# Fused spectral filter and feed-forward block: paired fold operations, four weight transfers in flight, and residual sums moved between engines

## The chip, the cores and the metric

The kernel runs on one core of one Trainium2 chip. The metric is the device time of one execution in microseconds; the figure quoted is a median over runs. A core has a matrix engine (PE, with its weight loads listed as PEld), a vector engine (DVE, VectorE), an activation engine (ACT, ScalarE), GpSimd (POOL), and a queue engine (SP) that issues nearly all transfers here. They run their own instruction streams in order and meet at semaphores.

## The reference

The input `x` has 2048 rows of 640 bfloat16 values. It is normalised once, and two branches read the result.

```
xn  = layernorm(x)                                   # over the 640 columns
A   = irfft2(rfft2(xn, (rows, cols)) * (w_r + i*w_i))  # filter of 2048 x 321 complex values
B   = gelu(xn @ w1 + b1) @ w2 + b2                   # 640 -> 1536 -> 640
out = x + A + B
```

## The kernel before

The 2048 rows are held as 16 tiles `c` of 128 rows; tile `c` has the rows `16p + c`. All Fourier transforms are matrix products with tables (`gtab`, `etab`, `mtab` forward; `ntab`, `getab`, `htab` back). The stages are:

1. **Normalise and fold** (lines 559 to 615). For each tile VectorE takes statistics (L563, L565), GpSimd makes `rstd` (L566, L567), and VectorE writes the normalised tile `xn` (L576). A transposed copy `xnT` is made through PE for the first eight tiles (L584, copied by L482 or L479) and by transfer for the last eight (L594). VectorE then folds the tile: two sums and differences of a half with the other half reversed (L601, 320 elements each), and four more of the result (L605, 256 and 64 elements). PE multiplies the folded tile with `gtab`, and the product is copied into `XW2`, which the trace calls `XW`.
2. **First product of the feed-forward branch** (`hps`, line 617 on): PE multiplies `w1` and `xnT` in blocks of 1, 1, 2, 4, 4 and 4 tiles, in all 360 matmuls of 128, 256 or 512 columns; ScalarE applies the gelu (L632). This is what fills PE while other stages wait.
3. **Forward transform and filter**: for each of 8 pairs PE runs `etab`, results are copied to `Xb`, PE runs `mtab`, results are copied to `Y`; VectorE multiplies `Y` with the filter weights `Wf` (L688, two per pair), adds the parts into `Z` (L693); small gathers make `Zs`; PE runs `ntab`; the result is copied to `XV`.
4. **Second product and inverse**: for each of 8 pairs `cp` PE runs `getab`, the result is copied into `Wf` (now free), VectorE unfolds it in two steps (L761, L766, two each), and PE adds the `htab` product. The second feed-forward product (`W,gT` in the trace, 24 matmuls of 320 columns for a tile) is the filler of this stage.
5. **Sums**: the first five tiles are "staged": their second product is done before the inverse is there. VectorE adds `b2` to it (L807), GpSimd adds the residual `x` (L810), and VectorE adds the inverse (L816). For the other eleven tiles GpSimd makes `x + b2` (L780), the `htab` product is accumulated onto the second product, and VectorE adds both (L800).

The order on every engine is not written by hand. A planner in the kernel (`Sched`) holds each operation with a guessed duration, a priority from `PRIO`, its buffers and its predecessors, lays the operations out in time on five engines, and emits that order with the semaphore waits it needs. An operation that may run on two engines is given to the one that the plan finds free first. Buffers come from pools (`Pool(n)` has n slots), so an operation can also have to wait for the last reader of a slot. Changing a duration or a dependency anywhere can therefore move operations everywhere.

The filter weights come in 18 transfers of 160.5 KB or less: four of rows of 10,272 bytes for each of `w_r` and `w_i`, then five each that bring the mirrored rows, in pieces of 642 bytes. Each is told to wait for an earlier one:

```
few.append(load(dst, src, B_w, nbytes, after=few[-DEPTH:][:1], rate=rate))
```

SP issues them in one queue with the transposes of tiles 8 to 15.

Of the kernel before, what the change touches and what calls it, by code (L numbers as in the profile page):

```python
# [10 lines left out]
ALU = mybir.AluOpType  # L11

S = 2048
D = 640
F = 1536
H2 = 320
# [82 lines left out]
def mm_us(n):  # L99
    return max(n / 2400.0 + 0.003, 0.0265)  # L100


def dve_us(n, rate=1.0):
    return 0.066 + n / 960.0 / rate


def act_us(n, ptr=0):
    return 0.052 + n / 1200.0 + 0.092 * ptr
# [8 lines left out]
PRIO = {"hps": 10, "gelu": 50, "pb": 70, "pc": 80, "filt": 85, "ipc": 90, "eps": 60, "fin": 40, "fst": 5}  # L117
# [6 lines left out]
DEPTH = 2  # L124
# [262 lines left out]
def bass_parallel_sum__spectral_gfnet__dense_activation_gelu__prompt_kernel(  # L387
# [21 lines left out]
    with ExitStack() as es:  # L409
# [3 lines left out]
        def view(t, off, dims):  # L413
            width = int(np.prod(t.shape[1:]))
            return bass.AP(tensor=t, offset=off, ap=[[width, 128]] + dims)
# [33 lines left out]
        XN, X1, XF = 0, 4 * D, 7 * D  # L449
# [13 lines left out]
        p_xn, p_x1, p_xf, p_xb, p_y, p_t, p_z, p_zs = Pool(8), Pool(3), Pool(4), Pool(2), Pool(2), Pool(2), Pool(2), Pool(2)  # L463
# [94 lines left out]
        norm_ops, ring_ops = [], []  # L558
        for c in range(16):
# [9 lines left out]
            xn, xf = Buf(f"xn{c}", p_xn), Buf(f"xf{c}", p_xf)  # L569

            def xnv(o, dims, xn=xn):
                return view(TT, XN + xn.slot * D + o, dims) if xn.slot < 4 else view(Zb, (xn.slot - 4) * D + o, dims)

            def xfv(o, dims, xf=xf):
                return view(TT, XF + xf.slot * D + o, dims)
            norm_ops.append(K.op([("dve", 0.36)], pr, lambda e, _, c=c, xnv=xnv: e.tensor_scalar(  # L576
                out=xnv(0, [[1, D]]), in0=view(XV, c * D, [[1, D]]), scalar1=mv[:, c, 0:1], scalar2=rstd[:, c:c + 1], op0=ALU.subtract, op1=ALU.mult),
                reads=[B_x[c], B_rs[c], B_mv], writes=[xn]))
            if c < BYPE:
# [6 lines left out]
                ring_ops.append(K.op([("pe", 5 * mm_us(128))], pr, xt, reads=[xn, B_id], writes=[tps]))  # L586
                if c == 0:
                    b1_column(ring_ops[:])
# [7 lines left out]
            x1 = Buf(f"xe{c}", p_x1)  # L596

            def x1v(o, dims, x1=x1):
                return view(TT, X1 + x1.slot * D + o, dims)
            for k, op in enumerate((ALU.add, ALU.subtract)):  # L600
                K.op([("dve", dve_us(H2, 2))], prf, lambda e, _, k=k, op=op, xnv=xnv, x1v=x1v: e.tensor_tensor(  # L601
                    out=x1v(H2 * k, [[1, H2]]), in0=xnv(0, [[1, H2]]), in1=xnv(D - 1, [[-1, H2]]), op=op), reads=[xn], writes=[x1])
            for k, op in enumerate((ALU.add, ALU.subtract)):
                for o_, o0, o1, n in ((128 * k, 0, H2 - 1, 128), (512 + 32 * k, 128, H2 - 129, 32)):
                    K.op([("dve", dve_us(2 * n, 2))], prf, lambda e, _, op=op, x1v=x1v, xfv=xfv, o_=o_, o0=o0, o1=o1, n=n: e.tensor_tensor(  # L605
                        out=xfv(o_, [[2 * n, 2], [1, n]]), in0=x1v(o0, [[H2, 2], [1, n]]), in1=x1v(o1, [[H2, 2], [-1, n]]), op=op),
                        reads=[x1], writes=[xf])
            aps = Buf(f"aps{c}", psum, 2, ZONE["aps"])
            ring_ops.append(K.op([("pe", 5 * mm_us(128))], prf, mms(lambda c=c, xfv=xfv, aps=aps: [
                (ps(aps.slot + j // 4, 128 * (j % 4), 128 * (j % 4) + 128), xfv(128 * j, [[1, 128]]), gtab[:, c, :], True, True) for j in range(5)]),  # L610
                reads=[xf, B_g], writes=[aps]))
            K.op([("dve", dve_us(640)), ("act", act_us(640))], prf,
                 copy(lambda c=c: view(XW2, 4 * c, [[2048, 5], [64, 32], [1, 4]]),
                      lambda aps=aps: PS[aps.slot // 2][:, 0:640].rearrange("p (j q r) -> p j q r", j=5, q=32)),
                 reads=[aps], writes=[B_xa[c]])
# [41 lines left out]
        for pair in range(8):  # L657
# [10 lines left out]
            cps_ops[pair] = [K.op([("pe", 4 * mm_us(KP) + 0.2)], PRIO["pc"] - pair / 5, mms(lambda pair=pair, cps=cps, xb=xb: [  # L668
# [75 lines left out]
        last, fin_ops, st_ops = [], {}, []  # L744
# [4 lines left out]
        for cp in range(8):  # L749
# [20 lines left out]
            for n in range(2):  # L770
# [8 lines left out]
                if not staged:  # L779
                    K.op([("pool", pool_us(640))], 50, lambda e, _, xr=xr, xov=xov: e.tensor_tensor(  # L780
                        out=xov(0, D), in0=xrt[:, xr.slot, :], in1=b2bc[:], op=ALU.add), reads=[xr, B_b2b], writes=[xo], after=[z_last])
# [11 lines left out]
                for hh in range(n_h):  # L793
# [9 lines left out]
                    if staged:  # L803
                        part = []
                        st_ops += second(hs, fps, hps_ops[block_of[c]], True)
                        add = Buf(f"st{c}")
                        K.op([("dve", dve_us(D))], 86, lambda e, _, xov=xov, fps=fps: e.tensor_tensor(  # L807
                            out=xov(0, D).rearrange("p (h n) -> p h n", h=2), in0=ps2(fps.slot, H2), in1=b2bc[:].rearrange("p (h n) -> p h n", h=2), op=ALU.add),
                            reads=[fps, B_b2b], writes=[add], after=all_hps)
                        K.op([("pool", pool_us(640) + 0.3)], 50, lambda e, _, xr=xr, xov=xov: e.tensor_tensor(  # L810
                            out=xov(0, D), in0=xov(0, D), in1=xrt[:, xr.slot, :], op=ALU.add), reads=[xr, add], writes=[xo], after=[z_last])
                        add = xo
# [11 lines left out]
                    K.op([("dve", dve_us(H2 * len(hs)))], 95, total, reads=[fps, add], writes=[os_])  # L824
# [34 lines left out]
```

## Time and profile before

| quantity | value |
|---|---|
| median of 13 runs | 168.27 us (165.93 to 170.16) |
| the profiled execution | 167.34 us, of which the span of the trace is 165.4 us |
| PE busy | 151.0 us (91% of the span) |
| VectorE busy | 120.5 us (73%) |
| ScalarE busy | 81.7 us (49%) |
| GpSimd busy | 36.4 us (22%) |
| granted clock of PE | 1.00 in every slice |

The profile page has the busy time of each engine, the span in 40 slices, the transfers by queue, the chain of work that ended last, and groups of equal instructions with their mean duration and what ended the idle time before them. The trace behind it answers with instructions in order of time, with waits, and with busy time in chosen windows. A duration in the trace contains the pipeline's tail, so for a run of equal instructions the distance from start to start is the better price.

### The profile page before, as it was taken

What the parts mean: (1) busy time and instruction counts of PE and PEld (TensorE: products, weight loads), DVE (VectorE), ACT (ScalarE), POOL (GpSimd) and SP (SyncE); (2) the same over time, 40 slices, a digit from 0 to 9 for tenths busy, and PEclk for the clock granted to TensorE, in tenths of its full rate; (3) what the DMA queues carried; (4) which work ended last, traced back from release to release, by engine and by line L of the source; (5) the groups of instructions that cost most, each with busy time, mean ns of one, the idle gap of its engine ahead of it and who ended that gap; (6) DMA issues with size and microseconds to landing.
All of it is one profiled execution on the core that took longest, in us unless ns stands there. A gap on an engine that the chain in (4) does not pass through costs nothing.

```text
span 165.4 us, 3694 instructions
## 1 busy us (share of the span) xinstructions
PE 151.0 (91%) x1485; PEld 94.9 (57%) x1485; DVE 120.5 (73%) x295; ACT 81.7 (49%) x163; POOL 36.4 (22%) x56
## 2 busy tenths in 40 slices
PE   6899999999999939999999999795699999999993
PEld 2489885444555514445556666563356777777772
DVE  3759999999982184967679988789999782923221
ACT  3299987786576838996889351313424010100000
POOL 1306233233200000000000000892703243333300
PEclk9999999999999999999999999999999999999999
DMA  3999944899995920050513000141524031211111
GB/s 109 352 384 394 296 119 116 135 130 123 87 133 86 159 74 0 0 162 0 162 29 133 0 0 4 40 119 44 164 73 159 23 117 65 84 40 40 42 63 55
DMA packets 18633, 17.86 MB, mean 108 GB/s; under 512 B 6712, under 2 KB 17336, under 8 KB 18488
## 3 DMA queue, kind: packets, MB, share of 16 engines
q1 hardware_dynamic: 18448, 17.59, 44.2%
q8 instruction: 11, 0.18, 0.5%
q10 hardware_dynamic: 168, 0.04, 0.1%
q14 instruction: 6, 0.05, 0.1%
HBM read 13.69 MB, written 2.62 MB: 99 GB/s over the span
## 4 chain that ended last, share of the span: by engine, by line
PE 40%; DVE 29%; DMA 18%; ACT 8%; issue 2%; SPq 2%; DVEq 0%
PE ps L472 40%; DMA Wf<-in_A_w_i_dram 7%; DMA Wf<-in_A_w_r_dram 6%; DVE stats L563 5%; DMA XV<-in_A_x_dram 5%; DVE T L688 4%; DVE T L605 3%; DVE T L576 2%; ACT Xb L479 2%; ACT Zs L479 2%; DVE Wf L761 2%; DVE Z L693 2%; DVE T L601 2%; DVE Wf L766 2%; DVE Y L482 1%
## 5 line engine op out<-in xcount | busy, mean ns | idle before, releaser
L472 PE MATMUL ps<-xnT,W 128*128 128x512 bf16 (+2 forms) x360 | 58.6, 309 | 1.3 <-DVE xnT L482 0.5
L472 PE MATMUL ps<-W,gT 128*128 128x320 bf16 x384 | 56.5, 299 | 0.3 <-DVE xnT L807 0.2
L472 PEld LDWEIGHTS ps<-W,gT 128*128 128x128 bf16 x384 | 36.7, 98 | 15.1 <-DVE xnT L807 0.8
L632 ACT ACTIVATE gT<-ps,b1col 128x512 bf16<-128x512 f32 (+2 forms) x72 | 37.1, 545 | 7.3 <-PE ps L472 6.7
L472 PEld LDWEIGHTS ps<-xnT,W 128*128 128x128 bf16 x360 | 28.1, 98 | 20.1 <-ACT gT L632 2.9
L800 DVE TENSOR_TENSOR ost<-ps,xo 128x640 bf16<-128x640 f32 (+1 forms) x12 | 9.2, 767 | 18.2 <-PE ps L472 18.2
L780 POOL TENSOR_TENSOR xo<-xr,b2bc 128x640 f32<-128x640 bf16 x11 | 16.1, 1466 | 24.7 <-DVE ost L800 24.7
L479 ACT ACTIVATE Wf<-ps 128x640 bf16<-128x640 f32 x12 | 8.0, 702 | 27.1 <-PE ps L472 24.9
L810 POOL TENSOR_TENSOR xnT<-xnT,xr 128x640 f32<-128x640 f32 x5 | 6.9, 1404 | 62.2 <-DVE Z L693 59.3
L563 DVE BATCH_NORM_STATS2 stats<-XV 128x6 f32<-128x320 bf16 x32 | 14.8, 474 | 3.3 <-DMA XV<-in_A_x_dram 3.3
L688 DVE TENSOR_TENSOR T<-Y,Wf 128x1288 bf16<-128x1288 bf16 x16 | 12.7, 828 | 4.1 <-ACT gT L632 3.6
L605 DVE TENSOR_TENSOR T<-T 128x256 bf16<-128x256 bf16 x64 | 11.7, 229 | 0.1
L761 DVE TENSOR_TENSOR Wf<-Wf 128x640 bf16<-128x640 bf16 x16 | 10.8, 702 | 0.2
L472 PE MATMUL ps<-Wf,htab 128*128 128x320 bf16 x32 | 7.2, 300 | 3.6 <-DVE Wf L766 3.4
L479 ACT ACTIVATE Xb<-ps 128x640 bf16<-128x640 f32 x11 | 9.3, 888 | 2.3 <-PE ps L472 2.3
L479 ACT ACTIVATE Zs<-Z 128x128 bf16<-128x128 bf16 (+1 forms) x33 | 6.4, 270 | 8.2 <-DVE Z L693 8.2
L479 ACT ACTIVATE XW<-ps 128x640 bf16<-128x640 f32 x13 | 9.0, 704 | 2.5 <-PE ps L472 2.2
L482 DVE CAST XV<-ps 128x640 bf16<-128x640 f32 x8 | 6.6, 824 | 5.0 <-PE ps L472 5.0
L566 POOL TENSOR_SCALAR ve<-mv 128x1 f32<-128x1 f32 x16 | 3.7, 233 | 29.5 <-DVE mv L565 29.5
L567 POOL TENSOR_TENSOR rstd<-ve,mhalf 128x1 f32<-128x1 f32 x16 | 9.4, 585 | 1.3
L472 PE MATMUL ps<-ntab,Z 64*128 64x128 bf16 x128 | 5.0, 218 | 4.5 <-ACT Xb L479 3.2
L601 DVE TENSOR_TENSOR T<-T 128x320 bf16<-128x320 bf16 x32 | 9.1, 294 | 0.0
(46 smaller groups left out, 147.6 us busy)
## 6 DMA issues: line engine op xcount, KB each, us to landing
W<-in_B_w_dram SPq DMA_DIRECT2D x6, 640.0 KB, 4.9
xr<-in_A_x_dram SPq DMA_DIRECT2D x16, 160.0 KB, 2.3
out_dram<-ost SPq DMA_DIRECT2D x15, 160.0 KB, 1.8
XV<-in_A_x_dram SPq DMA_DIRECT2D x7, 320.0 KB, 9.3
Wf<-in_A_w_r_dram SPq DMA_DIRECT2D x7, 160.5 KB, 5.0
Wf<-in_A_w_i_dram SPq DMA_DIRECT2D x7, 160.5 KB, 3.7
gtab<-c_G SPq DMA_DIRECT2D x1, 512.0 KB, 8.9
htab<-c_H SPq DMA_DIRECT2D x1, 512.0 KB, 10.8
```

What stands on the lines that cost most here:

```text
L472: ins = e.matmul(o_, lhsT=lw, rhs=rh, start=st, stop=sp_)
L479: return e.activation(dst(), src(), ACT.Copy, scale=scale)
L482: return e.tensor_copy(dst(), src())
L563: K.op([("dve", 0.4)], pr, lambda e, _, c=c, h=h: e.bn_stats(stats[:, c, 6 * h:6 * h + 6], view(XV, c * D + H2 * h, [[1, H2]])), reads=[B_ ...
L567: K.op([("pool", 0.6)], pr, lambda e, _, c=c: e.tensor_tensor(out=rstd[:, c:c + 1], in0=ve[:, c:c + 1], in1=mhalf[:, c:c + 1], op=ALU.pow) ...
L601: K.op([("dve", dve_us(H2, 2))], prf, lambda e, _, k=k, op=op, xnv=xnv, x1v=x1v: e.tensor_tensor(out=x1v(H2 * k, [[1, H2]]), in0=xnv(0, [[ ...
L605: K.op([("dve", dve_us(2 * n, 2))], prf, lambda e, _, op=op, x1v=x1v, xfv=xfv, o_=o_, o0=o0, o1=o1, n=n: e.tensor_tensor(out=xfv(o_, [[2 * ...
L632: K.op([("act", act_us(s1 - s0, 1))], pr + PRIO["gelu"], lambda e, _, s0=s0, s1=s1, fc=fc, hps=hps: e.activation(gT[:, fc, s0:s1], ps(hps. ...
L688: t_ops[pair].append(K.op([("dve", dve_us(4 * KP, 2))], pr, lambda e, _, k=k, Y=Y, TB=TB, pair=pair: e.tensor_tensor(out=view(TT, TB.slot ...
L761: K.op([("dve", dve_us(D, 2))], pr + 2, lambda e, _, k=k, op=op, yo=yo, y2=y2: e.tensor_tensor(out=view(Wf, Y2 + y2.slot * 2 * D + (H2 - 1 ...
L780: K.op([("pool", pool_us(640))], 50, lambda e, _, xr=xr, xov=xov: e.tensor_tensor(out=xov(0, D), in0=xrt[:, xr.slot, :], in1=b2bc[:], op=A ...
L800: return e.tensor_tensor(out=ost[:, os_.slot, a:b].rearrange("p (h n) -> p h n", h=len(hs)), in0=ps2(fps.slot, H2)[:, hs[0]:hs[-1] + 1, :] ...
```

## The change

Five things change together.

- **Folds over two tiles.** Tiles are folded in pairs. L601 becomes two instructions of 2 x 320 elements, L605 becomes four of 2 x 256 and 2 x 64, for every two tiles. The slots of `xn`, of the first fold and of the second fold now hold two tiles each: four pair slots of `xn` (it had eight single ones), two of each fold's result.
- **Weights four deep.** `DEPTH` goes from 2 to 4: a filter transfer waits for the one four places earlier.
- **Staged tiles on VectorE.** Residual plus bias of the five staged tiles is made by VectorE ahead of the product (`xpb`, priority 20, once the first product is through), and the product is then added to it; the GpSimd addition L810 is gone.
- **GpSimd paced.** The eleven GpSimd additions of tile `c` wait for the output sum of tile `c - 4`.
- **A planned duration.** The `mtab` step is planned with 0.36 us instead of 0.2 us of extra time, and the staged second products are gated on all of the first product.

```
-DEPTH = 2
+DEPTH = 4
+PACE = 4
...
-        p_xn, p_x1, p_xf, p_xb, p_y, p_t, p_z, p_zs = Pool(8), Pool(3), Pool(4), Pool(2), Pool(2), Pool(2), Pool(2), Pool(2)
+        p_xn, p_x1, p_xf, p_xb, p_y, p_t, p_z, p_zs = Pool(4), Pool(2), Pool(2), Pool(2), Pool(2), Pool(2), Pool(2), Pool(2)
...
             for k, op in enumerate((ALU.add, ALU.subtract)):
-                K.op([("dve", dve_us(H2, 2))], prf, lambda e, _, k=k, op=op, xnv=xnv, x1v=x1v: e.tensor_tensor(
-                    out=x1v(H2 * k, [[1, H2]]), in0=xnv(0, [[1, H2]]), in1=xnv(D - 1, [[-1, H2]]), op=op), reads=[xn], writes=[x1])
+                K.op([("dve", dve_us(D, 2))], prf, lambda e, _, k=k, op=op, xnv=xnv, x1v=x1v: e.tensor_tensor(
+                    out=x1v(H2 * k, [[D, 2], [1, H2]]), in0=xnv(-D, [[D, 2], [1, H2]]), in1=xnv(-1, [[D, 2], [-1, H2]]), op=op), reads=[xn2], writes=[x12])
...
+                if staged:
+                    K.op([("dve", dve_us(D))], PRIO["xb"], lambda e, _, xr=xr, xov=xov: e.tensor_tensor(
+                        out=xov(0, D), in0=xrt[:, xr.slot, :], in1=b2bc[:], op=ALU.add), reads=[xr, B_b2b], writes=[B_xb], after=all_hps)
+                else:
                     K.op([("pool", pool_us(640))], 50, lambda e, _, xr=xr, xov=xov: e.tensor_tensor(
-                        out=xov(0, D), in0=xrt[:, xr.slot, :], in1=b2bc[:], op=ALU.add), reads=[xr, B_b2b], writes=[xo], after=[z_last])
+                        out=xov(0, D), in0=xrt[:, xr.slot, :], in1=b2bc[:], op=ALU.add), reads=[xr, B_b2b], writes=[xo],
+                        after=[z_last] + os_ops[max(c - PACE, 0):][:1])
...
-                        K.op([("pool", pool_us(640) + 0.3)], 50, lambda e, _, xr=xr, xov=xov: e.tensor_tensor(
-                            out=xov(0, D), in0=xov(0, D), in1=xrt[:, xr.slot, :], op=ALU.add), reads=[xr, add], writes=[xo], after=[z_last])
```

As the planner now lays it out, ten of the 512-column matmuls of the first product that stood ahead of the first `etab` step stand behind it (98 ahead before, 88 now); 64 matmuls of the second product stand ahead of the last `ntab` step instead of 92; five of the copies into `XW` after the start-up are on VectorE instead of three; and the transposed copy of tile 1 is on ScalarE, ahead of its table load.

## The prediction

> **What bounds the kernel.** I read first the busy row and the PE row of the slices, then the busy time by stage, then the chain of waits. PE is busy 151.0 of 165.4 us at a granted clock of 1.00, and the 512-column matmuls follow each other every 0.215 us (13 in 2.80 us). The change removes no matmul, so it can only move the 14.4 us in which PE has none. Busy time by stage (length, then PE, weight loads, VectorE, ScalarE, GpSimd) shows where they lie:
>
> ```profile
> 36.00:58.00 22.00, 21.63 (x174) 11.00 (x172) 14.57 (x55) 15.57 (x24) 2.57 (x7) 1.00 1.00 119
> 58.00:62.20 4.20, 1.37 (x7) 0.48 (x5) 3.62 (x7) 1.53 (x6) 0.00 (x0) 1.00 0.19 61
> 62.20:105.00 42.80, 41.47 (x512) 23.78 (x512) 33.81 (x59) 29.61 (x66) 0.93 (x1) 1.00 0.16 47
> 105.00:125.00 20.00, 15.23 (x176) 9.80 (x179) 18.15 (x26) 6.01 (x9) 10.91 (x9) 1.00 0.32 98
> 125.00:163.00 38.00, 37.81 (x305) 27.02 (x304) 19.34 (x32) 2.71 (x4) 11.06 (x8) 1.00 0.21 69
> ```
>
> 2.8 us are lost at 58 to 62, 1.3 in the filter stage, 4.8 in the inverse (105 to 125). The rest is the start (2.4, before the first tile is there), 2.6 behind the last matmul, and 0.5 scattered. After 125 PE is full: what is saved earlier reaches the end. The chain names the first loss:
>
> ```profile
> 49.34 4.47 DMA Wf<-in_A_w_i_dram
> 53.82 0.02 issue
> 53.84 4.12 DMA Wf<-in_A_w_i_dram
> 57.95 0.04 DVEq L370
> ```
>
> The first filter product (L688) starts at 58.13, when the last weight transfer has landed. VectorE had its input `Y` at 54.57. The inverse's loss is in the timelines of GpSimd and VectorE:
>
> ```profile
> 104.07 5.50 POOL L810 TENSOR_TENSOR xnT<-xnT,xr 128x640 f32<-128x640 f32 x4 [59.30 <-DVE Z L693]
> 109.53 3.28 POOL L780 TENSOR_TENSOR xo<-xr,b2bc 128x640 f32<-128x640 bf16 x2
> ```
>
> ```profile
> 104.17 1.42 DVE L482 COPY Zs<-Z 128x128 bf16<-128x128 bf16 x1
> 109.48 2.09 DVE L761 TENSOR_TENSOR Wf<-Wf 128x640 bf16<-128x640 bf16 x2
> 111.61 1.96 DVE L766 TENSOR_TENSOR Wf<-Wf 128x640 bf16<-128x640 bf16 x2
> 119.02 0.88 DVE L766 TENSOR_TENSOR Wf<-Wf 128x640 bf16<-128x640 bf16 x2
> ```
>
> GpSimd runs without a break from 104.07 to 112.81. Beside it, VectorE's `Zs` copy takes 1.42 us (0.22 elsewhere) and a pair of unfolds about 2.0 (0.88 at 119.02). PE waits 0.84 for that `Zs` copy, 1.96 for the first L766 and 1.41 for a later one, behind a pair of L761 that took 2.52 beside GpSimd's additions at 115.74 to 118.75.
>
> **Part 1, paired folds.** From the run of folds at 45.17, start to start: two L601 0.47, four L605 0.61, so 1.08 a tile, 2.16 for two. These fit 0.067 us an instruction and 1920 elements a microsecond. A pair then costs 2 x 0.40 + 2 x 0.334 + 2 x 0.134 = 1.74: 0.42 less. Seven pairs lie in VectorE's dense stretch (11.91 to 48.99): -2.9; two more copies into `XW` at 0.74: +1.5. VectorE ends near 47.6, its last fold near 46.9. The order now has ten 512-column matmuls fewer ahead of the first `etab` (50.84 before), so PE is there 2.15 us earlier; with the start's delay (part 5) at 49.3, and at the last `gtab` products near 47.7. So the fold gain is worth nothing by itself: PE is full beside it, which hides it, and 0.8 us of cover remain. Bounds: 0, or if the two-tile pattern ran at half rate, 1.33 us more a pair, 9.3 us, less the cover: 8.5. I take 0: L688 has as many loop levels and 1288 elements in 0.785, and L605 reads backwards.
>
> A wait comes with it: the normalisation of tile 12 takes the slot of pair 8/9 and waits for both transposes. In the new order 22 statistics (0.40), 11 aggregates (0.12), 10 normalisations (0.36), 6 copies (0.40 to 0.74) and 3.6 paired folds (1.74 a pair) stand between the arrival of tile 2 at 11.91 and it: 22.7 us, so VectorE is there at 34.7. The transpose of tile 9 would be issued near 31; median landing is 3.9 us and the longest 6.3, so 35.0 to 37.4. Everything on VectorE is queued behind it, and then the transposes behind these on SP, and the weights behind them. Cost to PE 0 to 1.6; I take 0.4, and set against it the 0.37 that PE waited for an `XW` copy at 40.74. Sum 0.
>
> **Part 2, weights four deep.** The first transfer still goes alone (lands 22.85), since the second waits for it at either depth. Then 17 transfers take 35 us, two at a time, each landing 2.8 to 5.7 us after issue, with the 16 transfer engines idle at 26 to 27 and 52.5 to 53. With four, SP waits less for landings and more for the transposes between them: the last transfer stands behind the transpose of tile 14, whose normalisation ends by the same count at 40.4. So: issue near 42, landing 4.1 later, 46. It is needed at 54.57 - 2.15 + 0.6 = 53.0. Bounds: 46, and 57.95 if the engines are full anyway. I take the early end (7 us of cover). In the old run the work from L688 to `ntab` ended at 62.20; 3.56 earlier it would have been there at 58.64, before PE ran dry at 59.25. So the whole gap goes: **-2.95**. What is late next is PE itself.
>
> **Part 3, staged sums on VectorE.** Five L810 (1.40 each) leave GpSimd, five additions of 640 elements with an f32 result come to VectorE. No such row; the nearest is L807 (same width, f32 result), 0.74 start to start; at double rate 0.40, at worst 0.82. I take 0.74: +3.7 us. All five stand between the `Y` copy of pair 4 and the last L693. The new order there has 5 copies (0.73 to 0.80 each: 3.8), 8 L688 (0.785: 6.3), 8 L693 (0.45: 3.6), 2 sums of L807's kind (1.5), gathers (0.4) and the five additions (3.7), 19.3 us; with 1.5 of waiting for PE's products and ScalarE's closing gathers (0.7) and a handover, 21.65. PE has 20 matmuls of 512 columns (4.3), three `etab` (2.7), three `mtab` (2.0), three `ntab` (2.3) and 64 of 320 columns (8.7), with handovers 20.3: it waits 1.35 for the last `ntab`. Before it waited 0.84 there, by the slow `Zs` copy, which GpSimd no longer disturbs. **+0.5**; bounds -0.84 (adds in idle time) and +2.9 (all 3.7 exposed).
>
> **Part 4, paced GpSimd.** With L810 gone and L780 waiting for the output sum four tiles back, GpSimd is still until the sum of tile 1. The first unfold then takes 2.55 from the end of `getab` to `htab` (0.83 + 0.80 + 0.80 + 0.1 of handover), under PE's filler of 3.2: the 1.96 and the 1.41 go. But the additions for tiles 5 and 6 now start when the sums of tiles 1 and 2 end, and the next instructions on VectorE behind these are unfolds of pairs 1 and 2, which PE waits for. [...] By the order, a PSUM read stands between sum and unfold in the first case, and PE has 12 filler matmuls (1.63) to run: I get 0.55 and 0.7 of waiting. **-3.37 + 1.25 = -2.1.** Later pairs have 24 matmuls a tile (3.3 us), which covers an addition, as after 125 now.
>
> **Part 5, start.** ScalarE now copies tile 1's transpose (0.70) before its table load (1.28), so the first gelu begins near 9.6, not at 8.80. PE, which waited for ScalarE at 9.23, has done five transposes more by then (0.28). Nothing later gives that back: PE is full. 0.5 to 0.8, **+0.6**. The longer plan for `mtab` only moves order.
>
> **Sum.** -2.95 + 0.5 - 2.1 + 0.6 = -3.95. The profiled execution took 167.34 us, 1.94 outside its span: 163.4 would be its time. The median of the runs is 0.93 above that execution, so **164.3 us**.
>
> **Rivals.** [...] (b) The weights do not come earlier, so the depth does not do what it says. PE then meets the same landing 1.55 us earlier and waits 4.5: +0.55, 168.8; from a landing at about 59 on it is slower by over 1%, by a microsecond for each. For it: mean transfer-engine share 1.00 from 36 to 58, and one transpose that took 6.3 us. Against it: the idle holes, and that each pair is served in step. (c) Slower: the two-tile folds run at half rate. Place: the fold stage, which ends at 56.9 instead of 47.6; price 8.5 on PE: 172.8. It decides from 0.9 us more a pair on, when the fold stage ends near 54 (4.0 of gain and 1.7 for one per cent, behind 0.8 of cover). Against it stand the rows of L688 and L605.
>
> **Chances.** Forecast 0.55 (its own range 161.3 to 166.5, from the bounds of parts 3, 4 and the landing), (a) 0.20, (b) 0.13, (c) 0.12. The runs spread so that about 1% can be told from no change. Faster by over 1% (under 166.6): the forecast and 0.08 of (a), 0.63. Within 1%: the rest of (a) and 0.08 of (b), 0.20. Slower: (c) and the late end of (b), 0.17. The range takes in (a) and most of (b): 161.3 to 169.8.
>
> **What would show it.** Right: no wait of PE between the first L688 and the first `ntab`; last weight landing near 46; fold instructions of 2 x 320 at 0.40 and 2 x 256 at 0.33 start to start; first gelu near 9.6; one PE wait of about 1.3 before the last `ntab`; unfolds at 0.48 but for one or two that start beside an addition. Wrong: the landing after 53.6; folds at 0.73; PE waits of 3 us or more either before the last `ntab` or in the inverse; any idle of PE beyond the first 10 us at the `gtab` products.

## The result, and the profile after

| | before | after |
|---|---|---|
| median of the runs | 168.31 us (165.93 to 170.16, 48 runs) | 166.28 us (164.69 to 167.85, 11 runs) |
| the profiled execution | 167.34 us, span 165.4 | 164.5 us, span 162.7 |
| PE busy | 151.0 us | 150.4 us |

The ratio after to before is 0.9919, 95% interval 0.9883 to 0.9954. The comparison behind this ratio leaves out runs well above the fastest of their kernel, so it differs a little from the quotient of the two medians. The change makes the kernel 0.8 per cent faster (1.2 to 0.5); 164.3 us, 2.4 per cent less, had been forecast. The profiled pair differs by 2.84 us. A second series of the changed kernel (run 14 below) gave 0.9863, interval 0.9781 to 0.9945.

Busy time by stage, in the columns of the table shown for before (start and end of the stretch, its length, then PE, weight loads, VectorE, ScalarE, GpSimd, granted clock, transfer share, GB/s). The transfer share is the mean busy share of the 16 transfer engines; it adds up the time of all packets under way, and passes 1 in three of the stretches below (1.15, 1.09 and 1.29). First the kernel before:

```profile
12.00:26.00 14.00, 13.88 (x180) 12.21 (x178) 14.00 (x53) 12.79 (x32) 4.95 (x13) 1.00 0.83 263
26.00:36.00 10.00, 10.00 (x62) 4.85 (x61) 10.00 (x45) 7.73 (x13) 3.90 (x10) 1.00 0.83 126
36.00:50.00 14.00, 13.63 (x90) 6.84 (x89) 12.86 (x53) 9.45 (x16) 2.57 (x7) 1.00 1.15 116
50.00:62.00 12.00, 9.37 (x91) 4.63 (x89) 5.34 (x9) 7.45 (x14) 0.00 (x0) 1.00 0.57 105
62.00:105.00 43.00, 41.47 (x512) 23.78 (x512) 33.81 (x59) 29.81 (x67) 0.93 (x1) 1.00 0.16 47
105.00:125.00 20.00, 15.23 (x176) 9.80 (x179) 18.15 (x26) 6.01 (x9) 10.91 (x9) 1.00 0.32 98
```

The changed kernel:

```profile
12.00:26.00 14.00, 13.59 (x179) 11.96 (x175) 13.34 (x41) 12.35 (x32) 6.20 (x14) 1.00 0.92 282
26.00:36.00 10.00, 9.18 (x57) 4.66 (x58) 9.59 (x30) 6.17 (x11) 3.65 (x8) 1.00 1.09 114
36.00:50.00 14.00, 12.03 (x79) 5.93 (x77) 12.33 (x37) 8.51 (x13) 2.62 (x6) 1.00 1.29 128
50.00:62.00 12.00, 11.99 (x131) 6.27 (x130) 7.68 (x12) 8.92 (x17) 0.00 (x0) 1.00 0.62 88
62.00:105.00 43.00, 41.99 (x522) 23.67 (x521) 35.69 (x62) 31.95 (x71) 0.00 (x0) 1.00 0.22 67
105.00:125.00 20.00, 17.94 (x174) 11.97 (x174) 19.04 (x31) 5.30 (x8) 5.76 (x4) 1.00 0.22 75
```

Length less PE's busy time is what PE lost. By the same stretches the kernel before lost 0.12, 0.00, 0.37, 2.63, 1.53 and 4.77 us, the changed one 0.41, 0.82, 1.97, 0.01, 1.01 and 2.06. The loss in front of the filter (50 to 62) is gone, the inverse (105 to 125) lost 2.7 us less, and the fold stage (12 to 50), which had lost 0.49, loses 3.20.

The chain that ended last no longer runs over `Wf` transfers. It now runs through the fold stage:

```profile
35.81 1.08 issue
36.89 0.45 DVE T L582
37.34 0.61 DVE T L617 x3
37.95 0.05 issue
38.00 5.06 PE ps L473 x30
43.06 0.02 issue
43.08 0.70 ACT gT L645
43.78 0.11 issue
43.90 16.28 PE ps L473 x144
```

PE's timeline has the three waits that belong to it (in the brackets: idle time before the instruction, and what ended it):

```profile
26.82 0.82 PE L473 MATMUL ps<-xnT,W 128*128 128x512 bf16 x3 [0.98 <-DVE xnT L483]
38.00 0.73 PE L473 MATMUL ps<-gtab,T 128*128 128x128 bf16 x10 [1.12 <-DVE T L617]
43.90 0.81 PE L473 MATMUL ps<-xnT,W 128*128 128x512 bf16 x3 [0.85 <-ACT gT L645]
```

At 36.89 VectorE begins the normalisation of tile 12 after standing still: it had to wait for a slot that the transpose of tile 9 still read, and this landed at 36.80. At 43.90 the profile names a gelu, which ended at 43.78; the transpose of tile 11, an input of the product, came last, at 43.81. Run 1 below settles which of the two it was: there the transpose lands at 39.05, and PE does not stop at this place. The queue of SP and the list of transfers (KB each, median us from issue to landing) show how long such a transpose takes:

```profile
37.01 2.52 SPq L601 DMA_TRANSPOSE xnT<-T  x2
```

```profile
xnT<-T SPq DMA_TRANSPOSE x6, 5.4
xnT<-Z SPq DMA_TRANSPOSE x2, 8.5
```

Tile 11's was issued at 37.01 and took 6.8 us. In the kernel before the median of the eight is 3.9.

In the inverse GpSimd is still until the output sum of tile 1, as predicted. Then its first two additions each meet a pair of unfolds. Its timeline, and VectorE's:

```profile
110.70 1.39 POOL L797 TENSOR_TENSOR xo<-xr,b2bc 128x640 f32<-128x640 bf16 x1 [65.34 <-DVE ost L831]
114.86 1.57 POOL L797 TENSOR_TENSOR xo<-xr,b2bc 128x640 f32<-128x640 bf16 x1 [2.77 <-DVE ost L831]
```

```profile
111.27 1.57 DVE L779 TENSOR_TENSOR Wf<-Wf 128x640 bf16<-128x640 bf16 x2
114.71 2.08 DVE L779 TENSOR_TENSOR Wf<-Wf 128x640 bf16<-128x640 bf16 x2
```

The pair of L779 takes 0.88 where nothing runs beside it. Behind the second of them PE waits 1.38 us.

### The profile page after: what moved, and what is told of

It reads as the page before. It is cut to its first block, busy times and chain, and to the rows that moved or that the text cites. A ratio compares the mean times of both kernels' runs of the same rounds, so it can differ in the third digit from the quotient of the medians.

```text
span 162.7 us, 3642 instructions
## 1 busy us (share of the span) xinstructions
PE 150.4 (92%) x1485; PEld 94.6 (58%) x1485; DVE 119.1 (73%) x251; ACT 80.5 (49%) x164; POOL 30.0 (18%) x51
## 4 chain that ended last, share of the span: by engine, by line
PE 51%; DVE 26%; POOL 6%; DMA 5%; issue 5%; ACT 4%; SPq 2%; DVEq 0%; ACTq 0%
PE ps L473 51%; DMA XV<-in_A_x_dram 5%; POOL rstd L573 5%; DVE T L701 5%; DVE stats L569 3%; DVE Z L706 3%; DVE xnT L794 2%; DVE xnT L825 2%; ACT Zs L480 2%; SPq L468 2%; POOL ve L572 1%; DVE T L617 1%; DVE T L582 1%; DVE ost L831 1%; DVE Wf L774 1%
## 5 line engine op out<-in xcount | busy, mean ns | idle before, releaser
L473 PE MATMUL ps<-xnT,W 128*128 128x512 bf16 (+2 forms) x360 | 57.9, 308 | 3.0 <-ACT gT L645 1.6
L645 ACT ACTIVATE gT<-ps,b1col 128x512 bf16<-128x512 f32 (+2 forms) x72 | 36.3, 549 | 8.2 <-PE ps L473 7.9
L569 DVE BATCH_NORM_STATS2 stats<-XV 128x6 f32<-128x320 bf16 x32 | 13.8, 468 | 4.8 <-DMA XV<-in_A_x_dram 4.8
L701 DVE TENSOR_TENSOR T<-Y,Wf 128x1288 bf16<-128x1288 bf16 x16 | 12.6, 826 | 0.4
L573 POOL TENSOR_TENSOR rstd<-ve,mhalf 128x1 f32<-128x1 f32 x16 | 10.4, 653 | 1.3
L480 ACT ACTIVATE XW<-ps 128x640 bf16<-128x640 f32 x11 | 7.4, 702 | 5.1 <-PE ps L473 5.1
L774 DVE TENSOR_TENSOR Wf<-Wf 128x640 bf16<-128x640 bf16 x16 | 9.1, 602 | 1.1 <-ACT Wf L480 0.8
L779 DVE TENSOR_TENSOR Wf<-Wf 128x640 bf16<-128x640 bf16 x16 | 9.0, 602 | 0.2
L483 DVE CAST XV<-ps 128x640 bf16<-128x640 f32 x7 | 5.8, 822 | 4.5 <-PE ps L473 4.5
L473 PE MATMUL ps<-getab,XV 128*128 128x160 bf16 (+1 forms) x128 | 8.6, 233 | 0.2 <-DVE Wf L483 0.2
L473 PE MATMUL ps<-etab,XW 128*128 128x160 bf16 (+1 forms) x128 | 8.6, 234 | 0.0
L582 DVE TENSOR_SCALAR T<-XV,mv,rstd 128x640 bf16<-128x640 bf16 x14 | 6.2, 444 | 2.5 <-issue 1.2
## 6 DMA issues: line engine op xcount, KB each, us to landing
Wf<-in_A_w_r_dram SPq DMA_DIRECT2D x7, 160.5 KB, 5.5
Wf<-in_A_w_i_dram SPq DMA_DIRECT2D x7, 160.5 KB, 5.8
```

Of the source, the lines that this page charges most:

```text
L473: ins = e.matmul(o_, lhsT=lw, rhs=rh, start=st, stop=sp_)
L480: return e.activation(dst(), src(), ACT.Copy, scale=scale)
L483: return e.tensor_copy(dst(), src())
L569: K.op([("dve", 0.4)], pr, lambda e, _, c=c, h=h: e.bn_stats(stats[:, c, 6 * h:6 * h + 6], view(XV, c * D + H2 * h, [[1, H2]])), reads=[B_ ...
L573: K.op([("pool", 0.6)], pr, lambda e, _, c=c: e.tensor_tensor(out=rstd[:, c:c + 1], in0=ve[:, c:c + 1], in1=mhalf[:, c:c + 1], op=ALU.pow) ...
L645: K.op([("act", act_us(s1 - s0, 1))], pr + PRIO["gelu"], lambda e, _, s0=s0, s1=s1, fc=fc, hps=hps: e.activation(gT[:, fc, s0:s1], ps(hps. ...
```

## The experiments

The tables give PE's idle time in us by stretch of the profiled execution ("fold" is 12 to 50, "filter start" 50 to 62, "filter" 62 to 105, "inverse" 105 to 125), the last landing of a filter weight, and the mean of the transposes from issue to landing. A wait that crosses the end of a stretch is divided between the two. Each kernel was timed beside the kernel before on the same chip.

### Which part makes the fold stage wait

Run 1 takes the depth out of the change, run 2 is the depth alone, run 3 takes the paired folds out.

```
# run 1, on the changed kernel          # run 2, on the kernel before
-DEPTH = 4                              -DEPTH = 2
+DEPTH = 2                              +DEPTH = 4
```

> The changed kernel with the filter transfers two deep again, all else kept. Theory (the new losses of the fold stage come from transposes that land late because four weight transfers share the transfer engines with them, and from pair slots that wait for these transposes): the transpose of tile 11 lands before PE asks for it, so the 0.85 us wait at 43.9 goes and the 1.1 us wait at 38.0 shrinks; in exchange the last weight lands near 57 and PE waits 2 to 4 us ahead of the first ntab. Net 0.5 to 2 us slower than the changed kernel, span near 164. Rival (the fold stage is bound by VectorE whatever the transfers do): both PE waits of the fold stage stay, the weight wait is added in full, span 166 or more.

> The kernel before with the depth alone changed to four. Theory: the last weight lands some microseconds before PE needs the filter product, the 2.8 us gap at 58 to 62 goes and everything behind it moves up; the inverse stage keeps its 4.8 us of waits. Span 162.5 to 163. Rival (transfer engines are full, so depth only makes the transposes late): the gap shrinks by less than 1 us or PE waits for transposes of tiles 11 to 15 instead; span 164.5 or more.

```
# run 3, on the changed kernel: normalisation and folds of single tiles, as before
-            if c % 2 == 0:
-                xn2, x12, xf2 = Buf(f"xn{c}", p_xn), Buf(f"xe{c}", p_x1), Buf(f"xf{c}", p_xf)
+            xn, xf = Buf(f"xn{c}", p_xn), Buf(f"xf{c}", p_xf)
...
```

> The changed kernel with folds of single tiles, eight single slots for the normalised tile and the old order of the fold stage; depth four, staged sums on VectorE and the pacing are kept. Theory (the paired folds cost about 2 us of PE waits in the fold stage and bring nothing): PE waits under 0.6 us between 12 and 50, the inverse keeps about 2 us of waits, span 159.5 to 160.5, so 2 to 3 us under the changed kernel. Rival (paired folds carry part of the gain, by ten matmuls moved behind the first etab): the filter stage or the inverse gets back what the fold stage saves, span within 0.7 us of the changed kernel's 162.7.

| kernel | idle 12 to 36 | 36 to 50 | filter start | transposes | last weight | median us, ratio |
|---|---|---|---|---|---|---|
| before (single folds, depth 2) | 0.12 | 0.37 | 2.63 | 4.3 | 57.95 | 168.31 |
| run 1 (pairs, depth 2) | 1.46 | 0.13 | 0.21, then one wait of 2.08 at 62.8 | 3.8 | 60.17 | 168.16, 1.0025 (0.9985 to 1.0064) |
| run 2 (single, depth 4) | 0.44 | 2.80 | 0.11 | 6.6 | 50.93 | 170.89 (4 runs, no ratio) |
| run 3 (single, depth 4, rest of the change) | 0.44 | 2.86 | 0.11 | 6.3 | 50.76 | 169.13, 0.9979 (0.9940 to 1.0018) |
| changed (pairs, depth 4) | 1.23 | 1.97 | 0.01 | 6.2 | 54.40 | 166.28, 0.9919 (0.9883 to 0.9954) |

Run 1 came out as its theory said, run 2 as its rival. Run 3 missed: the fold stage was to lose under 0.6 us without the pairs and lost 3.30. (PE ran at a clock of 0.50 for two stretches of 3.4 us in its profile, so its waits are compared, not its span.) The two parts cost in two different places. With pairs PE loses 1.2 to 1.5 us before 36, at either depth; with four weights in flight it loses 2.0 to 2.9 from 36 to 50, with pairs or without. Without the pairs the profile names the cause itself. PE's timeline in run 2, then in run 3:

```profile
43.30 1.24 PE L472 MATMUL ps<-xnT,W 128*128 128x512 bf16 x5 [2.75 <-DMA xnT<-T]
```

```profile
42.95 2.12 PE L473 MATMUL ps<-xnT,W 128*128 128x512 bf16 x5 [2.64 <-DMA xnT<-T]
```

So the depth takes the wait for the weights away and puts a wait of the same size for a transpose in its place, nineteen microseconds earlier (it ends at 43.30 in run 2; the old one ended at 62.20). Run 1's weights land even later than before's; its transposes are issued about 2 us sooner (25.9 to 44.5, before 27.9 to 46.4) and stand ahead of more of the weights.

### The slot that tile 12 waits for

```
-                xn2, x12, xf2 = Buf(f"xn{c}", p_xn), ...
+                xn2, x12, xf2 = Buf(f"xn{c}", p_xn, 1, (c // 2 % 4, c // 2 % 4 + 1)), ...
```

The four pair slots are used in turn, so that tile 12 takes the slot of an older pair.

> The changed kernel with the four pair slots used in turn, so that tile 12 takes a slot that tiles 4 and 5 left long ago; the order of every engine is the same, only that wait is gone. Theory: VectorE does not stop for 1.18 us ahead of tile 12, the PE wait of 1.12 us at 38.0 goes, and the end comes 0.8 to 1.2 us earlier (span 161.5 to 161.9). Rival: PE reaches the next block of the first product 1.1 us earlier and waits there for the transpose of tile 11, which lands near 43.8 as before; gain under 0.4 us.

Measured: 164.88 us median of 6 runs, ratio 0.9839 (0.9774 to 0.9905). But the profile gained nothing: span 162.8 against 162.7, idle time from 36 to 50 1.93 against 1.97. VectorE's stop at 35.8 and PE's wait at 38.00 are gone, and PE stands 1.81 us at 42.2 to 44.0 instead, for the same transpose of tile 11, which lands at 43.92. The rival was right: the slot wait was in the chain and yet worth nothing, because what PE met next, tile 11's transpose, set the same end. The better median is not explained by the span; its interval overlaps with that of the changed kernel, and the section on the clock below says what else differs between runs.

### Transposes and weights

Run 5 makes all sixteen transposes on PE, on the changed kernel. Run 6 has slots in turn and a depth of 3. Run 8 has slots in turn and ten transposes on PE.

```
# run 5         # run 6         # run 8
-BYPE = 8       -DEPTH = 4      -BYPE = 8
+BYPE = 16      +DEPTH = 3      +BYPE = 10
```

> The changed kernel with BYPE 16: all sixteen tiles are transposed on TensorE, so that no transpose shares the DMA engines with the filter weights. It measures by itself the step of the prediction that let the weights land at 46. Theory (the transposes and the weights share one rate, about 120 GB/s between 26 and 50 us, so four transfers in flight only lengthen each): without transposes the same bytes land by 44 to 48, and TensorE's idle time between 36 and 50 falls from 1.97 to under 0.8 us. Eight more tiles cost TensorE 8 x 0.44 = 3.5 us and give back about 1.5, so a profiled execution of 165.5 to 167. Rival (the weights' reversed rows of 642 bytes are slow by themselves): the last weight lands after 52 all the same.

> The changed kernel with its pair slots used in turn and DEPTH 3. Theory: the latency of a transfer follows the number in flight; a transpose takes 4.0 us on average with two, 6.3 with four, so about 5 here; tile 11's lands at about 41 and TensorE's idle time between 36 and 50 falls from 1.93 to under 1 us, while the last weight lands at 55 to 57 and costs at most 1 us at the filter. Span 162.0 to 163.0, time 163.7 to 164.8. Rival (the depth does nothing to the transposes, and the order of the paired tiles holds them back): idle time between 36 and 50 stays at 1.9 and the weights' wait is added, time 165.5 or more.

> The changed kernel with its pair slots used in turn and BYPE 10: the transposes of tiles 8 and 9 go to TensorE (2 x 0.44 = 0.9 us), six stay on the DMA engines. Theory (the transposes' queueing makes the wait of 1.8 us at 42 to 44): tile 11's transpose lands before 42, idle time between 36 and 50 under 1 us, the last weight at 51 to 53; net span 162.3 to 163.3. Rival (VectorE's order, with two copies more, sets the end of the fold stage): idle time between 26 and 50 stays at 2.5 or more and the span is 163.8 or more.

| run | idle 12 to 36 | 36 to 50 | filter start | transposes | last weight | span | ratio |
|---|---|---|---|---|---|---|---|
| 5: no transposes by transfer | 1.20 | 0.11 | 0.32 | none | 47.91 | 165.1 | 0.9893 (0.9827 to 0.9958) |
| 6: depth 3 | 1.50 | 0.13 | 2.93 | 4.9 | 56.59 | 164.0 | 0.9930 (0.9886 to 0.9973) |
| 8: six transposes by transfer | 1.17 | 3.27 | 0.05 | 6.6 | 50.44 | 165.9 (clock 0.99) | 0.9939 (0.9894 to 0.9984) |

Run 5 answers the prediction's step: with no transposes beside them the weights do land at 47.9, near the 46 that it named, and both waits are gone. PE pays for it with the extra work (busy 151.9 against 150.4 us), and the filter and the inverse wait 2.5 us more than in the changed kernel (2.84 and 2.74). Run 6's transposes came out as expected, but the weights' wait came back whole: PE, no longer held up in the fold stage, arrived earlier at the same wall. Run 8 missed: two transposes fewer, but the first two that remained were issued behind a row of weights and took 7.2 and 7.6 us; PE waited 3.06 for the second of them, tile 11's.

GB/s times length from 26 to 50 us bears on these. The kernel before moved 1.26 + 1.62 = 2.88 MB, run 1 2.82, run 6 2.89, run 2 2.83, the changed kernel 1.14 + 1.79 = 2.93, and run 5, without transposes, 2.89 (run 8, the exception, 2.61). PE's view of run 5:

```profile
26.00:36.00 10.00, 9.14 (x71) 1.00 0.89 128
36.00:50.00 14.00, 13.89 (x105) 1.00 1.01 115
```

Depth or not, about 120 GB/s came through in this stretch, while 260 to 284 came through from 12 to 26. The share of busy transfer time rose from 0.83 to 1.09 (26 to 36) and from 1.15 to 1.29 (36 to 50) for 2 per cent more bytes: more in flight, hardly more moved. The transposes' mean time from issue to landing went with it: 3.8 to 4.3 us with two weights in flight, 4.9 with three, 6.2 to 6.6 with four. If the rate is fixed, twice as many weights in flight only make every transfer take longer, the transposes among them; these figures fit that reading. Run 5 has the same rate without transposes, so it is not they that set it; what does (the mirrored weight rows of 642 bytes, or something else) was not taken apart.

### Where the balance is

Run 9 sends tiles 8 to 11 to PE (BYPE 12, slots in turn, depth 4). Run 10 does the same at depth 3 and loads two tables, not needed before the inverse, behind the weights. Run 12 does only the latter, on the kernel of run 7. Run 15 is BYPE 12 in the kernel before, at its depth of 2.

```
# run 9: BYPE = 12. run 15: BYPE = 12 on the kernel before. runs 10 and 12 (10 with BYPE 12 and DEPTH 3):
-        load(getab[:], const["GE"], B_ge, 204800)
-        load(b2bc[:], bass.AP(tensor=b2v.tensor, offset=b2v.offset, ap=[[0, 128], [1, D]]), B_b2b, 163840)
...
+        load(getab[:], const["GE"], B_ge, 204800)
+        load(b2bc[:], bass.AP(tensor=b2v.tensor, offset=b2v.offset, ap=[[0, 128], [1, D]]), B_b2b, 163840)
         load(htab[:].rearrange("p a b -> p (a b)"), const["H"], B_h, 524288)
```

> The changed kernel with its pair slots used in turn and BYPE 12: tiles 8 to 11, whose transposes TensorE waited for, go to TensorE; tiles 12 to 15 stay on the DMA engines. Theory (one budget of transfer time between 26 and 55 us): the last weight lands at 49 to 51.5, TensorE's idle time between 12 and 62 falls from 3.4 to 1.6 to 2.2 us, and TensorE works 0.7 to 1.0 us more (half of what sixteen tiles added, 1.5); span 162.0 to 163.0. Rival (with ten tiles the waits only moved to the later transposes, and they will again): idle time between 36 and 50 stays at 2 us or more, span 164 or more.

> As the run with twelve tiles transposed on TensorE, but with DEPTH 3 and the loads of getab and b2bc (368 KB, needed only by the inverse and the end) behind the filter weights instead of ahead of them. Theory (budget): at the 270 GB/s moved before 26 us the weights start 1.3 us earlier; the last lands at 48 to 51 in spite of the smaller depth, nothing waits for it, and transposes take 4 to 5 us: idle time between 12 and 62 us at most 1.8 us, span 161.8 to 162.8. Rival (depth sets the rate of the weights): the last weight lands after 53.5, a wait of 0.5 to 2 us at the filter, span 163 or more.

> The run of the inverse's part alone (folds of single tiles, DEPTH 2), with the loads of getab and b2bc behind the filter weights. Theory (budget): the weights start 1.3 us earlier, the last lands at 57.1 instead of 58.4, and TensorE's wait before the ntab products falls from 3.6 to 2.3 us; at full clock the span is 1.3 us under that kernel's, 161 to 163.7. Rival (with two in flight each transfer's latency sets the landing, and the transposes' times of issue are fixed): the last weight lands at 58 or later, wait 3.3 or more, no gain.

> The kernel before with one number changed, BYPE 12, at DEPTH 2. Theory (weights and transposes share one budget of transfer time): with four transposes instead of eight the last weight lands at 50 to 53 without more of them in flight, and the wait of 2.83 us before the ntab products goes without coming up elsewhere: idle time from 12 to 62 falls from 3.1 to under 1.2; TensorE works 0.7 to 1.0 us more; the inverse keeps its 4 to 5 us; span 163.5 to 164.6. Rival (two transfers in flight set the rate of the weights, as the prediction had it): the last weight lands after 55.5, wait of 1 us or more, span 165 or more.

| run | idle fold | filter start | transposes | last weight | span | median us, ratio |
|---|---|---|---|---|---|---|
| 9 | 1.04 | 0.00 | 5.1 | 48.56 | 163.4 (clock 0.99) | 164.28, 0.9819 (0.9760 to 0.9878) |
| 10 | 0.98 | 0.01 | 5.1 | 49.92 | 161.7 | 164.48, 0.9831 (0.9744 to 0.9918) |
| 12 | 0.49 | 2.13 | 4.2 | 57.54 | 162.6 | 164.89, 0.9846 (0.9784 to 0.9908) |
| 15 | 0.51 | 2.70 | 4.1 | 57.39 | 165.6 | 169.87, 1.0111 (0.9987 to 1.0235) |

Run 15 went against my theory of one budget. With four transposes fewer and two weights in flight, VectorE still waited for the last weight:

```profile
57.56 1.57 DVE L688 TENSOR_TENSOR T<-Y,Wf 128x1288 bf16<-128x1288 bf16 x2 [3.06 <-DMA Wf<-in_A_w_i_dram]
```

Only 2.31 MB moved from 26 to 50. Two transfers of 160.5 KB with 4.05 us each (mean of the last ten) give the weights 2 x 0.164 / 4.05 = 81 GB/s. So these runs show two limits: the number in flight, as the prediction had it (81 GB/s for the weights in run 15), and the 120 GB/s. The kernel before was near both (two in flight, 2.88 MB in 24 us): its transposes filled what the weights left. Raising the depth alone (run 2) or taking transposes away alone (run 15) therefore brings nothing, and both together (runs 9 and 10) take the waits away: 1.0 us lost from 12 to 62 instead of 3.2. The transposes on PE take most of this back (busy 152.0 us in run 10, 1.6 more), and run 10's span is 1.0 us shorter. Runs 9 and 10 differ in the depth and in the order of the two tables, and these were not separated. Run 12's last weight landed 0.9 us earlier than run 7's, and PE's whole wait there fell from 3.63 to 2.13 us, near the 2.3 expected.

### The inverse

Run 7 is what is left of the change without pairs and without depth. Run 11 takes away only the pacing.

```
# run 7: the kernel of run 3 with DEPTH = 2. run 11, on the changed kernel:
-                        after=[z_last] + os_ops[max(c - PACE, 0):][:1])
+                        after=[z_last])
```

> The changed kernel with the folds of single tiles and DEPTH 2: what is left of the change is the staged second products, residual plus bias on VectorE and the pacing of GpSimd's additions. The parts add: TensorE's idle time from 105 to 125 us is 2.0 to 2.5 as in the changed kernel (4.77 in the kernel before), that from 12 to 50 under 1, and the weights' wait of some 2.8 us is back; profiled execution 164.3 to 165.5 at full clock, ratio 0.983 to 0.995. Rival (the inverse gained only because the pairs and the depth moved it in time): idle time from 105 to 125 over 3.5 and a ratio of 0.997 or more.

> The changed kernel with GpSimd's additions of the tiles from 5 on waiting only for z_last, as in the kernel before, not for finished tiles. Theory (the gain of the inverse is GpSimd's collisions with VectorE's additions, moved apart by the staged sums and by the pacing): the first three additions run together right after z_last, beside VectorE's folds, and TensorE's idle time from 105 to 125 rises from 2.06 to between 2.6 and 3.8; span 163.2 to 164.2. Rival (what matters is only that the staged residuals left GpSimd): idle time from 105 to 125 stays within 0.3 of 2.06, span 162.4 to 163.0.

Run 7: the inverse loses 1.95 us, with 3.07 in front of the filter and 0.86 in the fold stage, where the kernel before had 2.63 and 0.49. Its four runs (164.0 to 167.76; median 167.32) allow no ratio, and its profile has a stretch at half clock in the inverse; run 12, the same kernel but for two loads and at full clock throughout, loses the same 1.95. The gain of the inverse is there without the pairs and without the depth.

Run 11: 164.57 us, ratio 0.9839 (0.9780 to 0.9898), span 161.6. Both expectations missed: the idle time of the inverse does not rise, it falls from 2.06 to 0.52. GpSimd's and VectorE's timelines in run 11:

```profile
99.95 4.09 POOL L797 TENSOR_TENSOR xo<-xr,b2bc 128x640 f32<-128x640 bf16 x3 [54.92 <-DVE Z L706]
121.46 1.40 POOL L797 TENSOR_TENSOR xo<-xr,b2bc 128x640 f32<-128x640 bf16 x1 [17.41 <-DVE ost L818]
```

```profile
100.53 0.90 DVE L483 COPY Zs<-Z 128x128 bf16<-128x128 bf16 x1
111.67 0.88 DVE L779 TENSOR_TENSOR Wf<-Wf 128x640 bf16<-128x640 bf16 x2
114.41 0.88 DVE L779 TENSOR_TENSOR Wf<-Wf 128x640 bf16<-128x640 bf16 x2
```

The three additions that have free slots run in one piece at 100 to 104. They slow one gather (0.90 instead of 0.22, and PE waits 0.90 for it), and then GpSimd is away until 121.46: the unfolds that took 1.57 and 2.08 take 0.88. So neither pairs, depth nor pacing made the inverse faster. What is left is that the five L810 left GpSimd, together with the longer plan for `mtab` and the later second products, which no run separates from it. The pacing moves the other additions from a place where they cost 0.7 us to one where they cost 1.5.

The size of the gain depends on where the additions happen to fall. Runs 2 and 15 leave the inverse's code as it was and yet lose 2.89 and 2.98 there instead of 4.77. From 62 to 125, so that no wait falls out at the edge, the kernels with L810 on GpSimd lose 6.30 (before), 5.45 (run 2) and 5.14 (run 15), those without 4.03 (run 12), 3.07 (changed) and 2.22 (run 11).

### Both gains together, and the change once more

Run 13 is run 10 without pacing. Run 14 is the changed kernel again, beside it.

```
# run 13, on the changed kernel, with slots in turn and the two tables loaded late as in run 10
-DEPTH = 4
+DEPTH = 3
-BYPE = 8
+BYPE = 12
-                        after=[z_last] + os_ops[max(c - PACE, 0):][:1])
+                        after=[z_last])
```

> The run with twelve tiles transposed on TensorE, DEPTH 3 and late constants, and GpSimd's additions waiting for z_last alone. Theory (the two gains lie in different stages and add): TensorE's idle time from 12 to 62 stays near 1.0, from 62 to 105 it is 1.5 to 2.0, from 105 to 125 about 0.5; span at full clock 160.6 to 161.4, time 162.4 to 163.6, ratio 0.968 to 0.982. Rival (behind the inverse the end of the kernel is set by the output chain, which the pacing had put in order): span 161.7 or more.

> The changed kernel once more, so that its time stands beside the last two kernels on the same chip. Theory (its record with a ratio of 0.9919 came from a mean clock of 0.99 in most runs): at a clock of 1.0 the span is 162.5 to 163, ratio 0.984 to 0.992. Rival (the change is worth no more than its first measurement said): ratio 0.992 or more.

Run 13: 163.24 us (162.65 to 163.43, 6 runs), ratio 0.9757 (0.9714 to 0.9800). Run 14: 165.30 us (164.13 to 167.73, 6 runs), ratio 0.9863. PE in run 13, by stretch (PE, clock, transfer share, GB/s):

```profile
26.00:36.00 10.00, 9.41 (x70) 1.00 0.60 107
36.00:50.00 14.00, 13.72 (x95) 1.00 0.93 101
50.00:62.00 12.00, 12.00 (x138) 1.00 0.24 70
62.00:105.00 43.00, 41.29 (x516) 1.00 0.25 74
105.00:125.00 20.00, 19.48 (x188) 1.00 0.20 67
```

The waits are where they were expected: 1.1 us from 12 to 62, 1.7 in the filter, 0.5 in the inverse. The spans do not add, though: 161.4 against 161.7 in run 10 and 161.6 in run 11. Against run 11 PE waits 2.0 us less from 12 to 62 (1.1 instead of 3.1) and is busy 2.0 us more (152.1 instead of 150.1): the transposes on PE cost about what they save. Run 13 leads in the median, and none of its runs lost clock (last section). Its interval lies below 1 and below that of the changed kernel's first series; it overlaps with those of the second series and of runs 10 and 11.

## Why the prediction was right or wrong

**Sum: too large.** The forecast had two steps: 163.4 us for the profiled execution, and 0.93 more for the median. The profiled execution took 164.5, so the sum of -3.95 was -2.84; and the median lies 1.78 above it. By PE's idle time (the 0.74 us of the `Zs` wait that lie behind 105 in the kernel before are counted with the filter here, where the prediction had them):

| step | forecast | measured |
|---|---|---|
| start | +0.6 | first `gtab` product at 15.08 instead of 14.72, with two more small matmuls (0.06 each) ahead: about +0.2 |
| fold stage | 0 | +2.7 (0.49 to 3.20) |
| weights | -2.95 | -2.6 (2.63 to 0.01) |
| filter | +0.5 | -1.3 (2.27 to 1.01) |
| inverse | -2.1 | -2.0 (4.03 to 2.06) |

The filter came out 1.8 us better than forecast and hides most of what the fold stage lost. The rows add up to -3.0; PE's last product ended 2.76 us earlier.

**The step that failed is the fold stage's "Sum 0".** It had two terms. The wait for tile 12's slot was found, placed and priced (0 to 1.6, taken as 0.4), and was set against an `XW` wait that did go. It measured 1.12. What was not in the sum is that the same depth that speeds the weights slows the transposes: their landing was taken from the kernel before (3.9 median, 6.3 longest), and at depth 4 it is 6.2 on average, 6.8 for tile 11. With two in flight (run 1) the same folds brought PE to the first `etab` at 49.57, where the prediction had put it (49.3); with four it was there at 51.64. Rival (b) had this evidence in hand ("mean transfer-engine share 1.00 from 36 to 58, and one transpose that took 6.3 us") but asked only what it means for the weights. The second missing term is the later copy of tile 7's transpose in the paired order, 0.98 at 26.82; run 1 shows it at depth 2 too (1.2).

**The landing of the weights was wrong, and its effect right by luck.** 54.40 instead of 46; issued at 45.3, not 42, and 9.1 us on the way, not 4.1. At the planned pace the filter would have asked for it at 53.0 and waited 1.4. Because the fold stage had lost its 2.7 us, the first L701 started at 55.47, behind its `Y` copy, and nothing waited: one error covered the other. The premise (depth sets the weights' rate) holds only up to the 120 GB/s: run 5 landed at 47.91, run 15 at 57.39.

**Folds: right.** Two L613 start 0.40 apart, L617 of 512 elements 0.33; the half-rate rival is out. Two of them in VectorE's timeline:

```profile
47.34 0.88 DVE L613 TENSOR_TENSOR Y<-Z 128x640 bf16<-128x640 bf16 x2
```

That the gain behind them is worth nothing by itself is not shown separately. VectorE ended at 49.9, not 47.6: it stood still for 1.2 and 0.7 us.

**Staged sums: price right, place wrong.** One L794 is 0.82 us long, 0.74 start to start, as taken. But the last `ntab` waits 0.21, not 1.35: PE came later there, and the additions lay in VectorE's gaps. The additions cost nothing that shows, as the prediction's lower bound had it.

**Pacing: the collision right, the comparison missing.** PE waits 2.07 in all there (1.38, 0.29, 0.23, 0.17), where 1.25 of collisions and 0.7 of other waits had been left in the sum. The pairs that overlap an addition grow by 0.7 and 1.2 (1.57 and 2.08 against 0.88), no more than the 1.4 to 1.6 of one addition; in the kernel before, one L761 took 0.472 at the least and 1.684 at the most. No run shows the 0.55 and 0.7 of waiting that make up the 1.25, nor the bound of -0.6 (both additions of 1.40 waited for whole) that is in the range and in the 168.2 of rival (a), VectorE as the new bound: the longest single wait there was 1.38. What the prediction never asked is what the additions would cost without pacing: 0.7 us instead of 1.5 (run 11).

**The median.** That the median lies 0.93 us above the profiled execution was carried over from the kernel before without a reason. The changed kernel was profiled at a clock of 1.00, while 8 of its first 12 executions had a mean clock of 0.99. At a like clock the two kernels lie 2.35 us apart above 0.995 and 2.1 apart at 0.99 (numbers in the last section, over several series). How the other 0.85 us of the miss divides between the clock and the choice of the profiled execution stays open.

**The signs.** Two of the signs of being wrong came true: idle time of PE at the `gtab` products (1.12 us at 38.00), and the landing after 53.6.

## What to carry to other kernels

Before raising the number of transfers in flight, compare bytes moved per stretch, not busy share: here 26 to 50 us moved about 120 GB/s with two weights in flight or four, the transposes took 3.8 to 4.3 us on average with two and 6.2 to 6.6 with four, and one that is waited for (tile 11's) came late. Count the two limits separately, transfers in flight over latency (81 GB/s in run 15) and the total rate (120 GB/s here), and do not count on easing one while the other is as tight: run 2 eased the first and got a wait of 2.75 us for a transpose where the weights' had gone, run 15 made room under the second and came out at a ratio of 1.0111. And when an operation that disturbs others is moved, price the place it goes to as well as the one it leaves (the paced additions cost 1.5 us, those of run 11 0.7).

## What was not expected of the hardware

**In run 9 a wait of PE cost twice.** Runs of one kernel differ in the mean granted clock, in steps: of 84 runs of the kernel before, 26 at a clock above 0.995 have a median of 167.05 us, 44 at 0.99 one of 168.74, 13 at 0.98 one of 169.65, and one ran at 0.97. The changed kernel has 164.70 (8 runs above 0.995) and 166.64 (10 at 0.99). The profiles of runs 2, 3, 7, 8 and 9 caught six stretches at half clock (0.50). PE in run 9, by stretch (PE, clock, transfer share, GB/s), and its timeline:

```profile
115.00:117.00 2.00, 0.62 (x6) 1.00 0.29 72
117.00:119.00 2.00, 1.71 (x10) 0.74 0.38 136
119.00:121.00 2.00, 2.00 (x9) 0.50 0.45 152
121.00:123.00 2.00, 2.00 (x20) 0.91 0.00 0
```

```profile
116.64 0.45 PE L473 MATMUL ps<-Wf,htab 128*128 128x320 bf16 x2 [1.38 <-DVE xnT L825]
117.37 5.11 PE L473 MATMUL ps<-W,gT 128*128 128x320 bf16 x24 [0.29 <-DVE ost L831]
```

A wait of 1.38 us, and then 24 matmuls take 5.11 instead of 3.43: 1.7 us more, as much as lies between the first two medians above (1.69). All six stretches last 3.41 us. The waits in front of them were of 1.38 (run 9), 1.95 (runs 3 and 7), 1.96 (run 2), 2.64 (run 3) and 3.06 us (run 8).

Why one wait is hit and another is not can be read in part from the times. Every one of the six begins a whole number of steps of 3.413 us after the clock record of its profile begins: in run 9 the record begins at 5.31 and the half clock at 117.95, 33 steps later; in run 3 at 5.61, 43.16 (11 steps) and 118.25 (33), so that its two stretches lie 75.09 us apart, 22 steps. In the kernel before the record begins at 6.64 and shows half clock from 167.07 on, behind the last matmul, 47 steps later. Cut into such steps, the fourteen profiles that have a clock record give PE's idle time inside each. Of the seven steps with more than 1.9 us of it (1.95 to 2.64), five were followed by half clock; of the eight with 1.6 to 1.9, one was (run 9, 1.66); of all others, none. The 2.83 us of the kernel before fell across two steps, 1.88 and 0.95, and the clock stayed. So idle time inside one step sorts the cases better than the length of a wait, and on this reading the same wait can be hit or not by where the edge of a step falls. It does not sort them without exception, and no run tested it.

By kernel the share of runs that lost clock goes with the longest wait behind the first 10 us. With 1.35 us or less (runs 5, 11 and 13) none of 14 ran below 0.995; with 1.38 it was 10 of 18 (changed) and 3 of 8 (runs 9 and 10); with 1.81 to 2.13 (runs 1, 4 and 12) 16 of 30; with 2.64 to 3.63 (before and runs 2, 3, 6, 7, 8 and 15) 110 of 140. This is a correlation over these kernels.
